# Value sums of the pooled attention from the local attention's value tiles, by 0/1 products on the tensor engine

## The chip, the cores and the metric

The kernel runs on one core of one Trainium2 chip. The metric is the device time of one execution in microseconds (us). Engines: PE multiplies matrices (PEld loads its weights), DVE is the vector engine, ACT the scalar engine, POOL the general engine, SP issues most transfers. Sixteen DMA engines move the data. Each engine works through its own instructions in a fixed order and waits on semaphores for the others.

## What is computed

All arrays are f32. Attention is computed twice, once on means of four neighbouring tokens ("pooled") and once inside a band of seven tokens ("local"). The sum of both goes through a Fourier mixing, a norm and a feed-forward layer.

```
q, k, v = (8, 8, 576, 64)                      # batch, heads, tokens, dim
q_d, k_d, v_d = means over 4 tokens             # 144 groups
out_d = softmax(q_d k_d^T / 8) v_d              # pooled
out_l = softmax(q k^T / 8 where |i - j| < 4) v  # local
x = repeat(out_d, 4) + out_l                    # as (8, 576, 512)
u = x + real(fft(fft(x, axis=1), axis=2))
y = u + relu(norm(u) @ w1) @ w2                 # w1 512 x 2048, w2 2048 x 512
```

## The kernel before, in words

The attention and the mixing (`Pooled`, `Unit`, `Mix`) run batch by batch over the first 300 us or so; the feed-forward part takes the rest and keeps PE full with its own weights. The eight batches overlap: each is paced 20 schedule units after the one before.

A batch's local attention is five `Unit`s of 128 token columns. Each loads `qkT` (queries and keys of all heads, 512 KB) and `vaug` (values with a column of ones, two windows of 64 tokens by four pairs of heads, 260 KB), scores it on PE, takes maxima on DVE, exponentials on ACT, turns the result on PE, copies it on ACT, multiplies by `vaug` (`values`, tile `av`) and divides on DVE (`result`).

The pooled attention of a batch (`Pooled`) works in three parts. Its queries and keys are sums over four columns of each `qkT` (`sum_in`, L526 on DVE; L523 and L524 on POOL for the keys of batches 2 to 7), 144 groups. Its values are the tile `vsum`: four slices of `in_vg_dram` (every fourth token of the values, once more in DRAM) loaded on top of one another, the first by a plain transfer of SP's queue, the other three by accumulating transfers that POOL issues (`sum_v`, L360). The 16 groups beyond 128 are then laid out by ACT in four copies to `vd` (`spread`, L365). `values` multiplies with both (L428 with `vd`, L441 with `vsum`, tile `avd`).

The order on every engine is written out by hand: the table `AT` gives each step a time in schedule units, `at(...)` files it, and the steps are emitted sorted by that time. The times only set the order. Waits come from data, from the buffers of each tile (`NUM_V`, `NUM_QKT`) and from PSUM banks, which `bank` hands out by the filed time of the step that reads them. Behind the attention in the order, but among it in time, run the loads of the first feed-forward blocks (`ul`, `um`, `ud` into `ut`, accumulated by POOL's transfers at L868 and L874) and the decode of the first weights (a load to `raw`, then ACT, POOL and three steps of DVE on `wt`, then a cast on ACT and a difference).

Of the kernel before, what the change touches and what calls it, by code (L numbers as in the profile page):

```python
# [17 lines left out]
NUM_V, NUM_QKT, NUM_P = 3, 6, 2  # L18
# [6 lines left out]
POOL_SUMS = ((slice(0, 4), 0), (slice(4, 8), 1))  # L25
AT = {
    "pooled": (1.39, -0.67, -3.4, -4.0, -3.53),
    "mix": (18.69, 18.25, 18.08),
    "local_steps": (0.47, 2.18, 2.55, 4.76, 5.66, 7.44, 8.16),
    "pooled_steps": (0.21, 1.79, 2.89, 4.92, 5.63, 7.66, 9.61),  # L30
    "qk": (-14.26, 2.19),
    "sums": (-2.08, 0.13),
    "sum_v": (-14.82, -12.57, -2.25, 2.01),
    "load_v": (-1.96, 4.03),
    "store_pooled": (1.06, 0.8, 3.47),
    "crosses": ((1, 4.16), (2, 6.77), (0, 9.01)),
    "folds": ((3, 3.9), (1, 5.14), (2, 8.37), (0, 10.61)),
    "splits": (0.74, 1.1, 1.97),
    "z": (9.21, 9.92, 13.29, 13.75),
    "sequence": (12.93, 2.04, 0.82, 1.85),  # L40
# [3 lines left out]
    "decode": (50.58, 9.93, 6.96, 1.15, 1.87),  # L44
    "decode_steps": (-1.32, -0.39, 0.86, 2.11, 2.49),
    "add0": (62.59, 0.41, 6.0),
    "early": (3.29, 3.77),
    "constants": (10.75, 29.61),
    "waves": ((16.5, 0.16), (17.55, 0.92), (22.14, 0.9)),
    "waves_c": ((21.38, -3.88), (23.72, -1.16), (25.3, 7.97)),  # L50
    "qk1": (-16.47, 3.04),
    "sum_v1": (-19.42, -12.25, -4.44, 3.9),
    "qk0": (-8.34, 1.63),
    "sums0": (-0.4, 0.38),
    "sums1": (-2.05, 0.32),
    "load_v0": (-2.76, 5.2),
    "load_v1": (1.5, 3.84),
    "sum_v0": (-13.22, -6.45, -4.68, 5.69),
    "units0": (-2.71, -1.19, 4.29, 12.25, 17.39),
    "norms0": (88.98, -2.44, 95.16, 4.13),  # L60
    "add1": (75.6, 5.23, 15.18),
    "norms1": (146.64, 4.24, 0.79, 1.83),
    "keep": (25.6,),
    "shift": (0.5,),
    "pace0": (1.04, 1.21),
    "parts": (0.22, 5.36, 9.32),
    "parts0": (5.14, 8.37, 13.06),
    "spread": (11.49, 5.0),
# [48 lines left out]
def kernel(  # L117
# [4 lines left out]
    vg: bass.AP,  # L122
# [5 lines left out]
    c_signs: bass.AP,  # L128
    out: bass.AP,
# [13 lines left out]
    LQ = 32  # L143
    NSL = 3
# [126 lines left out]
    vds = [pd.tile([P, 2, 2, D + 1], F32, name=f"vd{i}") for i in range(2)]  # L271
    for x in vds:
        nc.gpsimd.memset(x, 0.0)
# [11 lines left out]
        "values": "result",  # L285
        "sequence": "sequence_low",
# [60 lines left out]
    class Pooled:  # L347
# [40 lines left out]
        def exps(self, i):  # L388
# [3 lines left out]
            sd = self.sd[i] = pd.tile([P, 2, 2, G], F32, name="sd", bufs=1)  # L392
# [6 lines left out]
        def transpose_p(self, i):  # L399
# [5 lines left out]
            for k in range(4):  # L405
                x = sd[:, k % 2 if i else 0, k // 2, G - LQ :]
# [10 lines left out]
        def values(self, i):  # L417
# [19 lines left out]
            for a in range(2 if i else HP):  # L437
                for hl, o in enumerate(av):
# [5 lines left out]
                        self.vs[:, 2 * hp + hl, :],  # L444
# [5 lines left out]
        def result(self, i):  # L450
# [48 lines left out]
    class Unit:  # L499
# [1094 lines left out]
```

## Time and profile before

| | us |
|---|---|
| median of 3 runs | 1092.33 (1091.62 to 1097.79) |
| profiled execution, device time | 1091.27 |
| its span | 1089.5 |

| engine | busy us | share of the span |
|---|---|---|
| PE | 1037.6 | 95% |
| PEld | 855.9 | 79% |
| DVE | 755.4 | 69% |
| POOL | 591.0 | 54% |
| ACT | 488.1 | 45% |

The shares are means over unlike stages, so the kernel is read in stretches: the first 62 us, in which the pipeline of batches fills, five batches up to 249 us, the last two with their mixing, and the feed-forward part, which is PE's from about 348 us on. A busy PE is not PE at its peak, since its small products count with the time that each takes to pass through.

### The profile page before, as it was taken

To read this page: it belongs to the slowest core of one execution; us is meant where nothing else is said; L and a number is where in the kernel's file an instruction comes from. 1 tells how busy PE (TensorE), PEld (TensorE's weight loads), DVE (VectorE), ACT (ScalarE), POOL (GpSimd) and SP (SyncE) were. 2 spreads that over 40 slices of the span, in tenths; PEclk is the share of its full clock that TensorE was granted. 3 is DMA by queue.
4 is the path that set the end of the run, shared out by engine and by line. 5 is a ranking of instruction groups with operands and counts; after the bars stand their busy time and mean duration, and the time that the engine had idled before them with its cause. 6 is when DMAs were issued, how large, how long until landed. Compare 5 with 4: busy or idle time off the path is not lost.

```text
span 1089.5 us, 22339 instructions
## 1 busy us (share of the span) xinstructions
PE 1037.6 (95%) x8060; PEld 855.9 (79%) x8060; DVE 755.4 (69%) x1579; ACT 488.1 (45%) x1355; POOL 591.0 (54%) x742
## 2 busy tenths in 40 slices
PE   5899888989999999989999999999999999999998
PEld 4687767768887888878878888888888888888886
DVE  5888779988888997662566557678557668555544
ACT  4776656767554442111144333445334345333331
POOL 2254846653355674635646894457695448334330
PEclk7799799999999999999999999999999999999999
DMA  9797999885445442948832792223693223322212
GB/s 292 215 281 238 238 282 265 211 249 167 145 144 155 136 142 74 263 137 192 185 116 67 174 189 82 69 64 123 172 201 90 80 65 103 112 77 64 73 39 77
DMA packets 107880, 164.73 MB, mean 151 GB/s; under 512 B 13331, under 2 KB 56165, under 8 KB 107770
## 3 DMA queue, kind: packets, MB, share of 16 engines
q1 hardware_dynamic: 87850, 135.39, 38.5%
q0 software_dynamic: 19920, 27.92, 15.8%
q8 instruction: 63, 1.03, 0.4%
q14 instruction: 47, 0.39, 0.1%
HBM read 123.81 MB, written 39.19 MB: 150 GB/s over the span
## 4 chain that ended last, share of the span: by engine, by line
PE 72%; DMA 10%; DVE 7%; POOL 3%; ACT 3%; issue 3%; SPq 1%; DVEq 0%; POOLq 0%; ACTq 0%
PE acc L1211 24%; PE product L1165 21%; PE hps L962 10%; DMA vsum<-in_vg_dram 5%; PE acc L980 3%; PE acc L981 3%; PE acc L982 3%; DMA qkT<-in_qk_dram 2%; PE y L721 1%; PE tpn L919 1%; PE mix L767 1%; ACT sb L560 1%; PE avd L441 1%; DMA raw<-in_wq_dram 1%; DMA x<-rest 1%
## 5 line engine op out<-in xcount | busy, mean ns | idle before, releaser
L1211 PE MATMUL acc<-w,h 128*128 128x512 f32 x1152 | 288.4, 390 | 0.0
L1100 POOL TENSOR_TENSOR w<-w 128x256 fp32r<-128x256 f32 x168 | 187.0, 1300 | 163.8 <-ACT w L1096 151.4
L1211 PEld LDWEIGHTS acc<-w,h 128*128 128x128 f32 x1152 | 215.5, 188 | 44.4
L1216 DVE TENSOR_TENSOR ut<-acc,ut 128x512 f32<-128x512 f32 x96 | 66.1, 689 | 75.0 <-PE acc L1211 74.4
L1165 PE MATMUL product<-x_t,w 128*128 128x512 f32 x432 | 110.2, 390 | 0.6 <-ACT raw L1176 0.6
L1176 ACT COPY raw<-product 128x512 f32<-128x512 f32 x72 | 42.2, 586 | 139.5 <-PE product L1165 139.5
L962 PE MATMUL hps<-unT,w1h 128*128 128x512 f32 x384 | 103.2, 391 | 0.0
L1191 ACT ACTIVATE h<-raw 128x512 fp32r<-128x512 f32 x72 | 45.5, 632 | 125.9 <-DVE raw L1183 125.9
L1216 DVE TENSOR_TENSOR more_tokens<-acc,more_tokens 128x512 f32<-128x512 f32 x96 | 66.1, 688 | 43.6 <-PE acc L1211 42.3
L1165 PEld LDWEIGHTS product<-x_t,w 128*128 128x128 f32 x432 | 80.8, 188 | 18.2 <-ACT raw L1176 1.5
L1183 DVE TENSOR_TENSOR raw<-product,raw 128x512 f32<-128x512 f32 x72 | 49.6, 690 | 56.5 <-PE product L1165 30.2
L1118 POOL TENSOR_TENSOR w<-w,w 128x512 fp32r<-128x512 f32 x48 | 82.0, 1813 | 9.8 <-ACT w L1114 9.8
L962 PEld LDWEIGHTS hps<-unT,w1h 128*128 128x128 f32 x384 | 71.5, 188 | 14.6
L970 DVE SCALAR_TENSOR_TENSOR hl<-hps,hh 128x512 fp32r<-128x512 f32 x48 | 32.8, 685 | 65.1 <-ACT hh L966 65.1
L980 PE MATMUL acc<-w2h,hh 128*128 128x512 f32 x192 | 76.2, 397 | 0.7 <-DVE ut L986 0.7
L982 PE MATMUL acc<-w2h,hl 128*128 128x512 f32 x192 | 75.2, 392 | 0.0
L981 PE MATMUL acc<-w2l,hh 128*128 128x512 f32 x192 | 75.2, 392 | 0.0
L1165 PE MATMUL product<-x_b,w 128*128 128x512 f32 x288 | 73.3, 390 | 0.0
L1165 PE MATMUL product<-x_two,w 128*128 128x512 f32 x288 | 73.1, 390 | 0.0
L560 ACT ACTIVATE sb<-sc,mx 128x64 f32<-128x64 f32 x320 | 69.8, 329 | 1.3
L966 ACT ACTIVATE hh<-hps 128x512 fp32r<-128x512 f32 x48 | 28.3, 591 | 91.9 <-PE hps L962 91.9
L904 POOL TENSOR_TENSOR rstd<-rstd,mhalf 128x1 f32<-128x1 f32 x36 | 22.3, 618 | 84.3 <-DVE rstd L903 77.6
(176 smaller groups left out, 2313.4 us busy)
## 6 DMA issues: line engine op xcount, KB each, us to landing
w<-ws SPq DMA_DIRECT2D x168, 128.0 KB
qkT<-in_qk_dram SPq DMA_DIRECT2D x40, 512.0 KB
raw<-in_wq_dram SPq DMA_DIRECT2D x50, 256.0 KB
w<-ws SPq DMA_DIRECT2D x48, 256.0 KB
vaug<-in_vw_dram SPq DMA_DIRECT2D x40, 260.0 KB
ul<-x SPq DMA_DIRECT2D x8, 1024.0 KB
vsum<-in_vg_dram POOLq DMA_DIRECT2D x24, 325.0 KB, 7.5
out_dram<-ut SPq DMA_DIRECT2D x24, 256.0 KB
```

Source lines behind the costliest of these rows:

```text
L560: nc.scalar.activation(out=self.sb[:, hp, h2], in_=sc[:, hp], func=AF.Exp, scale=0.125, bias=self.mx[:, h2, hp : hp + 1],)
L962: nc.tensor.matmul(hps, a[:, c, :], unT[:, x, c, :], start=(i == 0), stop=(i == len(mms) - 1))
L980: nc.tensor.matmul(acc, hh, w2h, start=start, stop=False)
L981: nc.tensor.matmul(acc, hh, w2l, start=False, stop=False)
L982: nc.tensor.matmul(acc, hl, w2h, start=False, stop=stop)
L1100: nc.gpsimd.tensor_sub(out=w[:, HN:], in0=w[:, HN:].bitcast(F32), in1=w[:, :HN].bitcast(F32))
L1118: nc.gpsimd.tensor_sub(out=x, in0=x.bitcast(F32), in1=h.bitcast(F32))
L1165: nc.tensor.matmul(ps, w[:, a, c], x[:, b, c], start=begin and i == 0, stop=i == len(mms) - 1, skip_group_check=not begin,)
L1183: nc.vector.tensor_add(out=x, in0=self.ps[p, "z" if out == (0, 0) else "y"], in1=x)
L1191: nc.scalar.activation(out=self.hidden(p, out, 0), in_=x, func=AF.Relu)
L1211: nc.tensor.matmul(acc, a, b, start=n == 0, stop=n == len(mms) - 1)
L1216: nc.vector.tensor_add(out=u, in0=self.accs.pop((p, t)), in1=u)
```

## The change

The copy of the values in DRAM, its four transfers per batch and the four copies to `vd` go. Instead a constant `groups` (0/1, 160 KB) is loaded once; the step `group_values` multiplies it with the batch's five `vaug` tiles on PE, which gives sums over four tokens in three PSUM banks, and `copy_values` brings them to `vsum` on ACT. So that each `vaug` gives its own 32 groups, the pooled keys get 159 places in place of 144 (`KEY_SUMS`); a group that occurs twice gets values from one place and zeros at the other. All keys' sums of a batch are thus made for 159 places, and scores, maxima and exponentials are 159 wide. The five `vaug` of a batch are needed together, so there are five buffers (before: three) and they are loaded earlier (`load_v`). Most numbers of `AT` for the steps of the attention, the mixing and the first loads are new; of these only those of the replaced steps are shown.

```diff
-NUM_V, NUM_QKT, NUM_P = 3, 6, 2
+NUM_V, NUM_QKT, NUM_P = 5, 6, 2
...
-POOL_SUMS = ((slice(0, 4), 0), (slice(4, 8), 1))
...
-    "sum_v": (-14.82, -12.57, -2.25, 2.01),
-    "load_v": (-1.96, 4.03),
+    "load_v": (-11.565, 4.0),
+    "groups": (10.6, 11.771),
...
-    vds = [pd.tile([P, 2, 2, D + 1], F32, name=f"vd{i}") for i in range(2)]
-    for x in vds:
-        nc.gpsimd.memset(x, 0.0)
+    groups = pd.tile([P, NPAIR, 2, LQ], F32, name="groups")
+    nc.sync.dma_start(out=groups.rearrange("p m n g -> p (m n g)"), in_=c_groups)
+    none = pd.tile([P, LQ], F32, name="none")
+    nc.gpsimd.memset(none, 0.0)
...
-        def sum_v(self, r):
-
-            if r == 0:
-                self.vs = pd.tile([P, H + 2, D + 1], F32, name="vsum", bufs=2)
-            eng = nc.gpsimd if r else nc.sync
-            how = {"accum_op": ALU.add} if r else {}
-            eng.dma_start(out=self.vs.rearrange("g h d -> g (h d)"), in_=vg[self.b, r], **how)
-
-        def spread(self):
-            for k in range(4):
-                r = slice(k * LQ, k * LQ + LQ)
-                nc.scalar.copy(out=vds[self.b % 2][r, :, k % 2], in_=self.vs[r, H:])
+        def group_values(self):
+
+            vas = [u.va for u in units[NPAIR * self.b : NPAIR * self.b + NPAIR]]
+            ps = self.vps = [bank("vsum")[:, : HP * (D + 1)] for _ in range(3)]
+            for n2 in range(2):
+                for k, m in enumerate(GROUP_UNITS[:4]):
+                    for h2 in range(2):
+                        r = slice(h2 * D, h2 * D + D)
+                        nc.tensor.matmul(
+                            ps[h2][k * LQ : k * LQ + LQ],
+                            groups[r, m, n2],
+                            vas[m][r, n2].rearrange("p h d -> p (h d)"),
+                            start=n2 == 0,
+                            stop=n2 == 1,
+                            skip_group_check=True,
+                        )
+            m = GROUP_UNITS[4]
+            for i in range(2):
+                for n2 in (0, 1, None):
+                    for a in range(2):
+                        for h2 in range(2):
+                            r, k = slice(h2 * D, h2 * D + D), 2 * h2 + a
+                            c = (D + 1) * (2 * i + (1 - a if n2 is None else a))
+                            nc.tensor.matmul(
+                                ps[2][k * LQ : k * LQ + LQ, c : c + D + 1],
+                                none[r] if n2 is None else groups[r, m, n2],
+                                vas[m][r, n2 or 0, 2 * i + a, :],
+                                start=n2 != 1,
+                                stop=n2 != 0,
+                                skip_group_check=True,
+                            )
+
+        def copy_values(self):
+            vs = self.vs = pd.tile([P, 3, HP, D + 1], F32, name="vsum", bufs=1)
+            for i, ps in enumerate(self.vps):
+                nc.scalar.copy(out=vs[:, i].rearrange("p h d -> p (h d)"), in_=ps)
...
-            s = sums[self.b]
+            q, k = sums[self.b]
             sps = self.sps[i] = [
-                bank("sp")[:, : (2 if i else 1) * G].rearrange("p (a g) -> p a g", g=G) for _ in range(2)
+                bank("sp")[:, : (2 if i else 1) * GK].rearrange("p (a g) -> p a g", g=GK) for _ in range(2)
             ]
             for a in range(2 if i else HP):
                 for hl, sp in enumerate(sps):
                     r = slice(hl * D, hl * D + D)
                     if i:
                         hp = 2 * i - 2 + a
-                        nc.tensor.matmul(sp[:, a, :], s[r, 0, hp, :P], s[r, 1, hp, :], start=True, stop=True)
+                        nc.tensor.matmul(sp[:, a, :], q[r, hp, :P], k[r, hp, :], start=True, stop=True)
                     else:
                         nc.tensor.matmul(
-                            sp[a * LQ : a * LQ + LQ, 0, :], s[r, 0, a, G - LQ :], s[r, 1, a, :], start=True, stop=True
+                            sp[a * LQ : a * LQ + LQ, 0, :], q[r, a, G - LQ :], k[r, a, :], start=True, stop=True
                         )
...
-            vd = vds[self.b % 2]
+            vd = self.vs[:, 2]
...
-                    v = vd[r, i - 1] if i else vd[r, a // 2, a % 2]
+                    v = vd[r, 2 * i - 2 : 2 * i] if i else vd[r, a]
...
-                        self.vs[:, 2 * hp + hl, :],
+                        self.vs[:, hl, hp, :],
...
-            times_v = AT[f"sum_v{b}" if b < 2 else "sum_v"]
-            for r in range(4):
-                at(pooled_at(b) + times_v[r], self.sum_v, r)
-            at(pooled_at(b) + AT["spread"][min(b, 1)], self.spread)
+            for d, fn in zip(AT[f"groups{b}" if b < 2 else "groups"], (self.group_values, self.copy_values)):
+                at(pooled_at(b) + d, fn)
...
-                sums[self.b] = pd.tile([P, 2, HP, G], F32, name="sums", bufs=1)
-            x = self.qkT.rearrange("p i h w -> p (i h) w")
-            to = sums[self.b].rearrange("p i h g -> p (i h) g")
-            for at0, g, n in SUMS[self.m]:
-                groups = x[:, :, at0 : at0 + 4 * n].rearrange("p h (g r) -> p h g r", r=4)
-                for h, pool in POOL_SUMS:
-                    if pool and self.b in POOL_BATCHES:
+                sums[self.b] = [
+                    pd.tile([P, HP, n], F32, name=f"sums_{x}", bufs=1) for x, n in (("q", G), ("k", GK))
+                ]
+            for i, places in enumerate((SUMS, KEY_SUMS)):
+                x, to = self.qkT[:, i], sums[self.b][i]
+                for at0, g, n in places[self.m]:
+                    four = x[:, :, at0 : at0 + 4 * n].rearrange("p h (g r) -> p h g r", r=4)
+                    if i and self.b in POOL_BATCHES:
                         two = p2.tile([P, HP, 32, 2], F32, name="two", bufs=1)[:, :, :n]
-                        nc.gpsimd.tensor_tensor(out=two, in0=groups[:, h, :, 0:2], in1=groups[:, h, :, 2:4], op=ALU.add)
-                        nc.gpsimd.tensor_tensor(out=to[:, h, g : g + n], in0=two[:, :, :, 0], in1=two[:, :, :, 1], op=ALU.add)
+                        nc.gpsimd.tensor_tensor(out=two, in0=four[:, :, :, 0:2], in1=four[:, :, :, 2:4], op=ALU.add)
+                        nc.gpsimd.tensor_tensor(out=to[:, :, g : g + n], in0=two[:, :, :, 0], in1=two[:, :, :, 1], op=ALU.add)
                     else:
-                        nc.vector.tensor_reduce(out=to[:, h, g : g + n], in_=groups[:, h], axis=AX.X, op=ALU.add)
+                        nc.vector.tensor_reduce(out=to[:, :, g : g + n], in_=four, axis=AX.X, op=ALU.add)
...
+    groups = np.zeros((2, W, 5, 2, 32))
+    for k, m in enumerate(GROUP_UNITS):
+        taken = {}
+        for at0, first, n in KEY_SUMS[m]:
+            for g in range(n):
+                tokens = [SPANS[m][at0 + 4 * g + r] for r in range(4)]
+                taken.setdefault(min(tokens) // 4, (first + g - (P - 1 if k == 4 else k * 32), tokens))
+        for g, (slot, tokens) in taken.items():
+            if g in MINE[m]:
+                n2 = min(n for n in range(2) if set(tokens) <= set(SPANS[m][STARTS[m][n] :][:W]))
+                for t in tokens:
+                    groups[:, SPANS[m][STARTS[m][n2] :].index(t), m, n2, slot] = 1.0
+    groups = groups.reshape(P, -1)
...
+MINE = [range(0, 30), range(30, 58), range(58, 87), range(87, 115), range(115, 144)]
+KEY_SUMS = [[(0, 0, 32)], [(0, 32, 32)], [(0, 128, 16), (65, 144, 15)], [(0, 64, 32)], [(0, 96, 32)]]
+GROUP_UNITS = (0, 1, 3, 4, 2)
 SUMS = [[(0, 0, 32)], [(16, 32, 28)], [(12, 60, 12), (65, 129, 15)], [(0, 99, 30)], [(4, 72, 27)]]
```

Where the instructions stand now. First SP, at the program's start: `ident` and `mask` are constants, `qkT` and `vaug` the loads of the first units. Before:

```order
L191 DMA ident<-in_c_ident_dram 128x128
L264 DMA raw<-in_c_mask_dram 128x128
L360 DMA vsum<-in_vg_dram 128x650
L506 DMA qkT<-in_qk_dram 128x1024 x4
L510 DMA vaug<-in_vw_dram 128x520
L506 DMA qkT<-in_qk_dram 128x1024
L360 DMA vsum<-in_vg_dram 128x650
L510 DMA vaug<-in_vw_dram 128x520
L506 DMA qkT<-in_qk_dram 128x1024 x2
L510 DMA vaug<-in_vw_dram 128x520
```

Now, the same place:

```order
L190 DMA ident<-in_c_ident_dram 128x128
L263 DMA raw<-in_c_mask_dram 128x128
L271 DMA groups<-in_c_groups_dram 128x320
L527 DMA qkT<-in_qk_dram 128x1024 x4
L531 DMA vaug<-in_vw_dram 128x520
L527 DMA qkT<-in_qk_dram 128x1024
L531 DMA vaug<-in_vw_dram 128x520
L527 DMA qkT<-in_qk_dram 128x1024
L531 DMA vaug<-in_vw_dram 128x520
L527 DMA qkT<-in_qk_dram 128x1024
L531 DMA vaug<-in_vw_dram 128x520
L527 DMA qkT<-in_qk_dram 128x1024
```

The first slices of `vsum` for two batches are gone, and the fifth `vaug` (one row further) stands behind eight loads of `qkT`.

Second PE, in the fourth batch: `sp`, `tp` and `avd` are the pooled scores, their transposes and the pooled result, `mix` the mixing of an earlier batch, `av` the local result. Before:

```order
L767 MATMUL mix<-chanm,yl 128x258
L767 MATMUL mix<-chanm,yh 128x258 x2
L767 MATMUL mix<-chanm,yl 128x258
L767 MATMUL mix<-signs,yz 128x258
L589 MATMUL av<-vaug,pT 64x65 x16
L428 MATMUL avd<-vd_149,ptd_2245 32x65 x8
L441 MATMUL avd<-vsum,ptd_2243 32x65 x8
```

Now:

```order
L402 MATMUL sp<-sums_k,sums_q 128x159 x4
L429 MATMUL tp<-ident,sd 128x128 x2
L432 MATMUL tp<-ident,sd 32x128 x4
L363 MATMUL vsum<-vaug,groups 32x260 x16
L378 MATMUL vsum<-vaug,groups 32x65 x8
L378 MATMUL vsum<-vaug,none 32x65 x4
L378 MATMUL vsum<-vaug,groups 32x65 x8
L378 MATMUL vsum<-vaug,none 32x65 x4
L611 MATMUL av<-vaug,pT 64x65 x16
L767 MATMUL yz<-seqm,z 2x290 x8
L453 MATMUL avd<-vsum,ptd_2505 32x65 x8
L466 MATMUL avd<-vsum,ptd_2503 32x65 x8
```

The 40 new products stand one local `av` and one mixing product ahead of the first pooled result that needs them; everything behind them on PE waits with them for the batch's fifth `vaug`.

Third POOL, in the fifth batch: `ut` are token loads of the first feed-forward block, `two` and `sums` the keys' sums, `wt` a decode step. Before:

```order
L221 TENSOR_SCALAR wt<-wt 128x256
L868 DMA ut_110<-ud_57 128x1x512
L360 DMA vsum<-in_vg_dram 128x650
L523 TENSOR_TENSOR two<-qkT 128x256
L524 TENSOR_TENSOR sums<-two 128x4x32
L868 DMA ut_111<-ud_57 128x1x512
L523 TENSOR_TENSOR two<-qkT 128x4x56
```

Now:

```order
L220 TENSOR_SCALAR wt<-wt 128x256
L896 DMA ut_113<-um_73 128x2x256
L890 DMA ut_110<-ud_57 128x1x512
L545 TENSOR_TENSOR two<-qkT 128x256
L546 TENSOR_TENSOR sums_k<-two 128x4x32
L890 DMA ut_111<-ud_57 128x1x512
L545 TENSOR_TENSOR two<-qkT 128x256
```

The accumulating transfer of `vsum` is gone from between them; the sums are 128 x 256 wide for every unit but the third.

## Rows read from the trace of the kernel before

**Rows 1.** Stretches: length, busy us of each engine (instructions), PE clock, DMA share, GB/s

```profile
0.00:62.00 62.00, 45.72 (x861) 35.05 (x862) 41.97 (x131) 40.69 (x145) 21.40 (x36) 0.78 0.86 251
62.00:249.00 187.00, 164.87 (x2873) 135.85 (x2874) 157.19 (x481) 126.59 (x464) 110.72 (x167) 0.95 0.91 252
249.00:278.70 29.70, 28.80 (x505) 23.89 (x504) 26.12 (x89) 22.80 (x85) 11.60 (x16) 1.00 0.48 145
180.00:200.00 20.00, 15.92 (x305) 12.91 (x294) 19.05 (x57) 13.22 (x47) 11.44 (x15) 1.00 0.96 272
```

The engines stand in the order PE, PEld, DVE, ACT, POOL.

**Rows 2.** The page's chain that ended last, shares of the span by engine

```profile
PE 72%; DMA 10%; DVE 7%; POOL 3%; ACT 3%; issue 3%; SPq 1%; DVEq 0%; POOLq 0%; ACTq 0%
```

**Rows 3.** DMA queues, 0 to 310 us: packets, MB, share; issues, KB, us to landing

```profile
q1 hardware_dynamic: 29430, 58.39, 55.9%
q0 software_dynamic: 7504, 13.24, 25.4%
...
vsum<-in_vg_dram POOLq DMA_DIRECT2D x24, 325.0 KB, 7.5
...
vsum<-in_vg_dram SPq DMA_DIRECT2D x8, 325.0 KB
```

**Rows 4.** Chain of waits, 0 to 100 us: start, us, what

```profile
1.65 3.14 DMA vsum<-in_vg_dram
...
22.53 4.89 DMA vsum<-in_vg_dram
```

**Rows 5.** Chain of waits, 100 to 260 us, same columns

```profile
97.29 8.99 DMA raw<-in_wq_dram
...
173.60 6.69 DMA qkT<-in_qk_dram
...
182.38 8.45 DMA vsum<-in_vg_dram
190.85 0.30 ACT vd L365
```

**Rows 6.** Waits of DVE and ACT, 62 to 249 us: us in total, times, longest

```profile
DVE wt L229 <- POOL wt L221: 6.5, 3, 2.9
DVE w2l L251 <- ACT w2h L246: 4.8, 2, 3.0
DVE sums L526 <- DMA qkT<-in_qk_dram: 4.3, 3, 1.7
...
DVE w1l L251 <- ACT w1h L246: 0.9, 1, 0.9
...
ACT vd L365 <- DMA vsum<-in_vg_dram: 6.6, 4, 3.0
```

**Rows 7.** Instructions by shape, 62 to 249 us; L526: one line, min/median/max ns

```profile
L386 DVE TENSOR_REDUCE mxd<-sp 128x2 f32<-128x288 f32 x20 | 8.1, 445 | 0.0
L386 DVE TENSOR_REDUCE mxd<-sp 128x1 f32<-128x144 f32 x10 | 2.5, 295 | 0.0
L365 ACT COPY vd<-vsum 32x130 f32<-32x130 f32 x20 | 6.0, 298 | 6.7 <-DMA vsum<-in_vg_dram 6.6
L395 ACT ACTIVATE sd<-sp,mxd 128x144 f32<-128x144 f32 x50 | 15.2, 381 | 0.5
L773 ACT COPY o<-mix 128x258 f32<-128x258 f32 x10 | 4.0, 398 | 0.0
L526 DVE TENSOR_REDUCE sums<-qkT x60: 336/605/676, 8.5 to 253.4; 128x128 f32<-128x512 f32 x10, 128x112 f32<-128x448 f32 x10, 128x48 f32<-128x192 f32 x10, 128x60 f32<-128x240 f32 x10
```

**Rows 8.** Small products on PE: chain rows, then timeline rows, start, us, shape

```profile
237.45 1.26 PE sp L377 x8
255.85 0.41 PE sp L379 x16
195.71 0.40 PE L428 MATMUL avd<-vd,ptd 64*32 64x65 f32 x16
196.03 0.39 PE L441 MATMUL avd<-vsum,ptd 128*32 128x65 f32 x11
```

More of the change, by code (lines that the diff above doesn't have):

```diff
@@ L24 @@
 PACE = 20
-POOL_SUMS = ((slice(0, 4), 0), (slice(4, 8), 1))
 AT = {
[L27 to L32, printed above, removed]
-    "sum_v": (-14.82, -12.57, -2.25, 2.01),
-    "load_v": (-1.96, 4.03),
[L35 to L40, printed above, removed]
+    "pooled": (1.39, -1.682, -3.279, -4.179, -3.53),
+    "mix": (18.504, 17.944, 18.064),
+    "local_steps": (0.745, 1.871, 2.694, 4.76, 5.66, 7.44, 8.214),
+    "pooled_steps": (0.946, 1.778, 2.89, 4.92, 5.63, 7.863, 9.169),
+    "qk": (-13.864, 2.19),
+    "sums": (-1.884, 0.239),
+    "load_v": (-11.565, 4.0),
+    "groups": (10.6, 11.771),
+    "store_pooled": (1.06, 2.553, 3.47),
+    "crosses": ((1, 4.16), (2, 6.524), (0, 9.01)),
+    "folds": ((3, 3.843), (1, 5.114), (2, 8.459), (0, 10.61)),
+    "splits": (0.74, 1.175, 1.966),
+    "z": (9.21, 10.197, 12.281, 13.303),
+    "sequence": (12.804, 2.04, 0.954, 1.943),
     "mixed": (21.86, 2.32, 0.37, 0.44, 1.73, 2.55),
@@ L43 @@
     "ffn": (2.14, 1.64),
[L44 to L47, printed above, removed]
+    "decode": (50.58, 9.93, 8.429, 1.15, 1.87),
+    "decode_steps": (-1.32, -0.304, 0.86, 2.11, 2.73),
+    "add0": (61.253, 1.204, 6.32),
+    "early": (3.061, 4.713),
     "constants": (10.75, 29.61),
[L49 to L63, printed above, removed]
+    "waves": ((15.301, 0.16), (17.286, 0.92), (20.944, 2.831)),
+    "waves_c": ((20.094, -5.127), (23.72, 2.255), (27.466, 7.97)),
+    "qk1": (-21.509, 3.04),
+    "groups1": (10.6, 11.544),
+    "qk0": (-8.402, 1.336),
+    "sums0": (-0.4, 0.469),
+    "sums1": (-5.128, 0.365),
+    "load_v0": (-4.18, 2.691),
+    "load_v1": (-9.0, 4.333),
+    "groups0": (12.057, 12.6),
+    "units0": (-4.673, -1.19, 4.29, 12.25, 17.39),
+    "norms0": (92.56, -2.44, 93.504, 4.13),
+    "add1": (84.678, 5.23, 15.674),
+    "norms1": (139.931, 4.201, 3.347, 1.845),
+    "keep": (25.544,),
     "shift": (0.5,),
     "pace0": (1.04, 1.21),
-    "parts": (0.22, 5.36, 9.32),
-    "parts0": (5.14, 8.37, 13.06),
-    "spread": (11.49, 5.0),
+    "parts": (4.6, 8.372, 12.084),
+    "parts0": (5.14, 8.37, 11.66),
 }
@@ L128 @@
     c_signs: bass.AP,
+    c_groups: bass.AP,
     out: bass.AP,
@@ L143 @@
     LQ = 32
+    GK = P + LQ - 1
     NSL = 3
@@ L285 @@
         "values": "result",
+        "group_values": "copy_values",
         "sequence": "sequence_low",
@@ L391, in exps @@
             nc.scalar.mul(out=mx, in_=mx, mul=2.0**-7)
-            sd = self.sd[i] = pd.tile([P, 2, 2, G], F32, name="sd", bufs=1)
+            sd = self.sd[i] = pd.tile([P, 2, 2, GK], F32, name="sd", bufs=1)
             for hl, sp in enumerate(self.sps[i]):
@@ L405, in transpose_p @@
             for k in range(4):
-                x = sd[:, k % 2 if i else 0, k // 2, G - LQ :]
+                x = sd[:, k % 2 if i else 0, k // 2, GK - LQ :]
                 nc.tensor.matmul(rest[k * LQ : k * LQ + LQ, 0], x, ident, start=True, stop=True)
@@ L454, in result @@
             for hl, o in enumerate(av):
-                nc.vector.tensor_scalar(
-                    out=rs[:, hl], in0=o[:, :, D], scalar1=1e-9, scalar2=4.0, op0=ALU.add, op1=ALU.mult
-                )
+                nc.vector.tensor_scalar_add(out=rs[:, hl], in0=o[:, :, D], scalar1=4e-9)
             nc.vector.reciprocal(out=rs, in_=rs)
@@ L1496, in _constants @@
     signs[[0, 1, 32, 33]] = [1.0, -1.0]
-    out = {"c_ident": ident, "c_mask": mask, "c_seq": seq, "c_chan": chan, "c_signs": signs}
+    groups = np.zeros((2, W, 5, 2, 32))
[11 more added lines that the diff above has]
+    groups = groups.reshape(P, -1)
+    out = {"c_ident": ident, "c_mask": mask, "c_seq": seq, "c_chan": chan, "c_signs": signs, "c_groups": groups}
     out = {n: np.ascontiguousarray(a, dtype=np.float32) for n, a in out.items()}
@@ L1533, in _arrays @@
     both = np.pad(both, [(0, 0)] * 5 + [(0, pad)])
+    both[..., SEQ:] = both[..., SEQ - pad : SEQ][..., ::-1]
     data["qk"] = np.stack([both[..., s] for s in SPANS], axis=1).reshape(B, NPAIR, P, -1)
@@ L1539, in _arrays @@
     data["vw"] = np.pad(rows, [(0, 0)] * 6 + [(0, 1)], constant_values=1).reshape(B, NPAIR, P, -1)
-    groups = v.reshape(B, HEADS, 2, SEQ // 8, 4, DIM)
-    groups = np.concatenate([groups[:, :, 0], groups[:, :, 1, ::-1]], axis=2)
-    groups = np.pad(groups, [(0, 0)] * 4 + [(0, 1)], constant_values=0.25)
-    rest = np.zeros((B, HEADS, 32, 4, DIM + 1), groups.dtype)
-    rest[:, :, 16:] = groups[:, :, P:]
-    rest = rest.reshape(B, 2, 2, 2, 32, 4, DIM + 1).transpose(0, 5, 3, 2, 4, 1, 6).reshape(B, 4, P, 2, DIM + 1)
-    groups = np.concatenate([groups[:, :, :P].transpose(0, 3, 2, 1, 4), rest], axis=3)
-    data["vg"] = groups.reshape(B, 4, P, -1)
     w1, w2 = (np.asarray(inputs[n]) for n in ("moe_w_ch1", "moe_w_ch2"))
```

1 line of the change is left out of this document (removed).

## The prediction

> **What bounds the kernel now.** I read the stretches first [rows 1]. The whole change lies in the attention stage, so the reader should look at three of them. In the first 62 us (up to the first batch's local store) nothing is near full except the DMA engines, 0.86 busy. In the next 187 us, five batches at 187 / 5 = 37.4 us each, three things are close together: DMA 0.91, PE 164.9 / 187 = 0.88, DVE 157.2 / 187 = 0.84. The batch from 249 to 278.7 us is the useful comparison: its loads are over, DMA falls to 0.48, and a batch takes 29.7 us with PE at 28.8 / 29.7 = 0.97. So the middle batches are held back by something that the late batch does not have, and loads are the first suspect. The chain of the whole program gives DMA 10% [rows 2], and half of that is the transfers of `vsum`, the value sums that the change removes.
>
> Next the DMA queues of the first 310 us [rows 3]. The accumulating transfers are issued by POOL on q0: 13.24 MB there take 25.4% of 310 us, that is 78.7 us of all 16 engines, or 5.94 us per MB. On q1 58.39 MB take 55.9%, 173.3 us, or 2.97 us per MB. An accumulated megabyte costs twice a plain one.
>
> Then where these transfers are waited for. The first batch's four follow one another from 1.65 us to 22.53 + 4.89 = 27.4 us [rows 4]. Later, one piece of the chain is an 8.45 us `vsum` transfer that ends at 190.83 us and releases the four copies to `vd` [rows 5]. But the wait table of the middle [rows 6] shows how little of such a piece is idle time: ACT waits 6.6 us in four times for `vsum`. DVE, the engine with the least slack besides PE, waits 4.3 us for `qkT`, 6.5 us for the decode step of POOL and 4.8 + 0.9 us for ACT's decode casts. I count these 16.5 us as late transfers seen at second hand: a `raw` transfer of 256 KB took 8.99 us to land [rows 5], POOL issues accumulating transfers between the decode steps, and ACT's casts stand behind the `vd` copies. That is where I chose; only the 4.3 us end on a transfer directly.
>
> **The change, part by part.** *Transfers.* Per batch four of 128 x 650 x 4 bytes = 0.333 MB go. Eight plain ones cost 8 x 0.333 x 2.97 = 7.9 us of DMA time, 24 accumulating ones 24 x 0.333 x 5.94 = 47.5 us. The new table `groups`, 128 x 320 x 4 = 0.164 MB, costs 0.5 us. So 55 us of DMA time go, 6.9 per batch, of about 0.91 x 37.4 = 34 us. DMA stops being close to a bound; what a free engine is worth is set by what is late next.
>
> *Start.* The five `vaug` tiles take over from the four `vsum` transfers. Two plain and three accumulating transfers left the first 22 us: 2 x 0.333 x 2.97 + 3 x 0.333 x 5.94 - 0.5 = 7.4 us of DMA time. The group products must wait for the fifth `vaug`, which now stands behind eight `qkT` loads. I take about half, -4 us (bounds 0 and -8).
>
> *Middle.* All 16.5 us of DVE idle time above are taken as recovered. Bounds: 4.3 us, the direct wait, and 187 - 157.2 / 0.95 = 21.5 us, where DVE would be as full as from 180 to 200 us (19.05 of 20) [rows 1].
>
> *New work on PE.* Per batch 16 products of 64 x 32 by 260 columns and 24 by 65 columns. The trace counts each f32 product twice. Eight products of 64 x 32 by 144 columns (x16) took 0.41 us; eight by 65 columns ran from 195.71 to the next group at 196.03, 0.32 us, or 0.04 each [rows 8]. By columns the 16 cost 0.41 x 2 x 260 / 144 = 1.5 us, at most; scaled by the slope between the two rows, (0.41 - 0.32) / 8 / 79 per column, they cost 16 x (0.051 + 116 x 0.00014) = 1.1 us. I take 1.3, and 24 x 0.04 = 0.95 for the small ones: 2.25 us a batch, 18 in all. The far bound is the pace of the wide 64 x 128 products, four in 1.26 us for 144 columns [rows 8]: (16 x 260 + 24 x 65) x 1.26 / 4 / 144 = 12.5 us a batch, which the shape makes unlikely; I keep 4.5 us (twice mine) as bound. In the start PE idles 16 us of 62, which hides two batches' worth. In the middle five batches bring 11.3 us and PE idles 22 us; with PE at 0.88 I put half on the path, +5.6. In the late, PE-full stretch one batch counts whole, +2.3. The Trainium skill (TensorEngine Tiling, Gotcha 1: PSUM Pressure) says that row tiles of different halves cannot use one PSUM bank at the same time; the small products of both halves write one bank, where the measured rows used two. By that rule they would cost about 0.95 us a batch more, half of it on the path, and the sum would be near 1081; no row before shows it.
>
> *DVE.* Ten maxima per batch get 159 columns for 144. Two against one segment is 445 - 295 ns for 144 columns [rows 7], 1.04 ns a column, so 10 x 15 x 1.04 = 0.16 us a batch, 1.3 us in all. In batches 0 and 1 the twelve sums of keys grow by 15/144: 12 x 0.605 x 0.104 = 0.8 us [rows 7]. Together +2, on the path since DVE is nearly full.
>
> *ACT.* Four `vd` copies at 298 ns, 1.19 us, become three copies of 128 x 260, priced like `o`, 128 x 258 at 398 ns: 1.19 us. Nothing. Ten exponentials get 15 more columns; 144 take 381 ns, so at most 10 x 15 x 381 / 144 = 0.4 us a batch, hidden by ACT's idle 60 us of 187. If ACT had no slack it would cost 3 us.
>
> *POOL and the buffers.* POOL loses 24 issues and gains a tenth in the key sums of six batches. It idles 76 us of 187, so nothing; were it full, the two would roughly cancel. The wait for `vsum` on ACT becomes a wait for PE. Three PSUM banks per batch are held between products and copies, one and a bit schedule units, among some fifty bank uses; I price that at nothing (bounds 0 to 2 us).
>
> *PE's clock.* In the middle the mean granted clock is 0.95 [rows 1]. It has two levels, 1.2 and 2.4 GHz, so PE spent 2 x 0.05 x 187 = 18.7 us at the lower one and lost half of that, 9.4 us of work; in the late batch, where PE idles 0.9 us, it is 1.00. If some of the 22 us of PE's idle time go, some of the 9.4 us comes back: I take -4 (bounds 0 and -9.4).
>
> *Order.* The moved times of the other steps have no row that prices them: 0, bounds -6 to +6.
>
> **Sum.** The profiled execution took 1091.27 us (span 1089.5 and 1.8 around it), 1.1 below the median of the runs. -4 (start) - 16.5 (DVE's idle time) + 5.6 + 2.3 (PE) + 2 (DVE) - 4 (clock) = -14.6, so 1077 us.
>
> **Rivals.** *More* (chance 0.20). With DMA out of the way DVE runs at 0.95 in the middle: (157.2 + 1.5) / 0.95 = 167, -20, and the start gives its -8: 1063 us. For it speaks the late batch, 29.7 us at low DMA. Against it: that batch decodes little and sums no keys.
>
> *The transfers were hidden anyway* (0.18). Only the direct wait goes, -4.3 and -2 at the start; the new work stays, +5.6 + 2.3 + 2, and the clock stays as it is: 1095 us. For it: ACT's waits for `vsum` are 6.6 us in all and 3.0 at most [rows 6], however long the transfer on the chain.
>
> *Slower* (0.12). The group products stand in PE's fixed order, and with them everything behind waits for the batch's fifth `vaug`. By the table this is loaded at 4 x 4.0 - 11.565 = 4.4 and used at 10.6 - 3.53 = 7.1 units after the batch begins, 2.6 units of 37.4 / 20 = 1.87 us, so 5 us. A `qkT` of 512 KB took 6.69 us to land, a `raw` of 256 KB 8.99 us [rows 5]. At 8.99 PE would stand 4 us in each of seven batches: 1077 + 28 = 1105 us. It cancels the gain from 14 / 7 = 2 us of wait per batch. Against it: those landings were measured with the DMA engines full.
>
> **How the numbers follow.** The forecast, 1077 us, has chance 0.50 and its own range 1068 to 1086. Range 1060 to 1097: all of the forecast, most of *more* (0.14) and of *hidden* (0.15), together about 0.8; the slower case and the far end of *more* stay out. A change of under 1% is about what a measurement of this kernel cannot tell from none; the border is 1081.4. Faster: 0.20 from *more* and three quarters of the forecast, 0.38, so 0.58. Slower: 0.09 of the slower case and 0.02 of the hidden one, 0.11. Same: the rest, 0.31.
>
> **What would show it.** Right: DMA busy near (0.91 x 187 - 5 x 6.9) / 174 = 0.78 in the middle, q0 at 13.24 - 8 = 5.2 MB, batches of 33 to 35 us, PE at 0.95 there, hardly any DVE wait on POOL's decode step. Products of `vsum` at 2 to 2.5 us a batch confirm the PE price. Wrong: DMA down and batches still at 37 us (hidden); PE waiting for `vaug` in front of the group products (slower); the first batch's store still near 62 us says that the start was not the transfers'. After 348 us nothing should change but the offset.

## The result and the profile after

The changed kernel took 1077.67 us (median of four runs, 1077.20 to 1080.11) against 1092.3 us before: ratio 0.986, 95% interval 0.9825 to 0.9895. A second set of six runs gave 1078.41 us and 0.9863 (0.9833 to 0.9893). So it is 1.4% faster, 14.6 us, and the forecast was 1077 us, 14.6 us down. The agreement is too good: several terms of the sum were wrong, and their errors cancelled, as the stages show.

Both profiled executions of the changed kernel are the longest of their sets (1080.11 and 1079.88 us), while the profiled one of before was 1.1 us under its median. Between the profiled spans there are therefore only 11.2 us to find (1089.5 to 1078.3).

The stretches of the kernel after, cut at the same places as [rows 1]: start, five middle batches, one late batch, the last batch. Columns: length, busy us of PE, PEld, DVE, ACT, POOL (instructions), PE clock, DMA share, GB/s.

```profile
0.00:60.10 60.10, 51.21 (x1044) 38.74 (x1048) 46.40 (x138) 42.98 (x153) 16.74 (x32) 0.80 0.65 226
60.10:238.50 178.40, 167.41 (x3251) 136.33 (x3244) 153.74 (x473) 121.95 (x446) 97.86 (x148) 0.98 0.78 222
238.50:268.40 29.90, 29.53 (x582) 24.46 (x584) 27.36 (x89) 21.34 (x79) 10.16 (x14) 1.00 0.41 132
268.40:287.80 19.40, 19.40 (x318) 17.44 (x315) 13.76 (x51) 11.78 (x43) 3.71 (x6) 1.00 0.30 100
```

The middle went from 187.0 us to 178.4, with DMA down from 0.91 to 0.78 and PE up from 0.88 to 167.41 / 178.4 = 0.94. DVE idles 24.7 us there, before 29.8. The late batch did not get shorter (29.7 to 29.9 us).

The DMA queues of the first 300 us (packets, MB, share of 16 engines), as in [rows 3]:

```profile
q1 hardware_dynamic: 28333, 55.73, 56.5%
q0 software_dynamic: 4048, 5.25, 10.3%
```

q0 fell from 13.24 to 5.25 MB. The transfers are gone as counted, and the page's chain (shares of the span) says the same: DMA 10% in [rows 2] is 3% now, PE 72% is 78%.

```profile
PE 78%; DVE 11%; issue 3%; DMA 3%; ACT 2%; SPq 2%; POOL 1%; DVEq 0%; POOLq 0%; ACTq 0%
```

What DVE waits for in the middle, 55 to 240 us (us in total, times, longest), against [rows 6]:

```profile
DVE rs L626 <- PE av L611: 7.5, 6, 2.1
DVE rsd L480 <- PE avd L466: 2.9, 5, 1.1
DVE mxd L411 <- PE sp L402: 2.7, 3, 1.3
...
DVE sums_q L548 <- DMA qkT<-in_qk_dram: 0.5, 1, 0.5
```

The waits on POOL's decode step (6.5 us before), on ACT's casts (4.8 + 0.9) and on `qkT` (4.3) are gone or small. In their place stand waits for PE: `av`, `avd` and `sp`, 13.1 us. DVE's idle time changed its cause more than its size.

The new products at full clock, two rows of the chain of waits (start, us, what): 16 wide products (L363, counted twice) and 24 small ones (L378).

```profile
222.49 1.04 PE vsum L363 x32
223.53 0.68 PE vsum L378 x48
```

That is 1.72 us, where 2.25 were forecast, but it is the quickest of the five middle batches. The slowest ran from its first product at 77.12 us to PE's next step at 79.61, 2.49 us (start, us, what):

```profile
77.12 1.66 PE L363 MATMUL vsum<-vaug,groups 64*32 64x260 f32 x30
...
79.61 0.70 PE L611 MATMUL av<-vaug,pT 64*64 64x65 f32 x32
```

Read in this way the five took about 2.1 us in the mean, 1.9 in the second profile (without waits in between), near the forecast.

### The profile page after: what moved, and what is told of

Its sections match the earlier page's. It is cut to its first block, busy times and chain, and to the rows that moved or that the text cites. A ratio compares the mean times of both kernels' runs of the same rounds, so it can differ in the third digit from the quotient of the medians.

```text
span 1078.3 us, 23547 instructions
## 1 busy us (share of the span) xinstructions
PE 1047.1 (97%) x8700; PEld 860.7 (80%) x8700; DVE 762.7 (71%) x1579; ACT 486.5 (45%) x1347; POOL 571.7 (53%) x717
## 4 chain that ended last, share of the span: by engine, by line
PE 78%; DVE 11%; issue 3%; DMA 3%; ACT 2%; SPq 2%; POOL 1%; DVEq 0%; POOLq 0%; ACTq 0%
PE acc L1233 24%; PE product L1187 21%; PE hps L984 8%; PE y L743 4%; PE acc L1002 3%; PE acc L1004 3%; PE acc L1003 3%; PE tpl L594 2%; PE av L611 2%; PE mix L789 1%; PE avd L466 1%; PE sc L563 1%; PE tpn L941 1%; PE sp L402 1%; PE tp L429 1%
## 5 line engine op out<-in xcount | busy, mean ns | idle before, releaser
L1122 POOL TENSOR_TENSOR w<-w 128x256 fp32r<-128x256 f32 x168 | 182.5, 1233 | 165.1 <-ACT w L1118 152.7
L1205 DVE TENSOR_TENSOR raw<-product,raw 128x512 f32<-128x512 f32 x72 | 49.6, 689 | 55.6 <-PE product L1187 30.5
L1218 DVE SCALAR_TENSOR_TENSOR h<-raw,h 128x512 fp32r<-128x512 f32 x72 | 64.3, 893 | 1.0 <-ACT h L1213 0.7
```

Source lines behind the costliest of these rows:

```text
L1122: nc.gpsimd.tensor_sub(out=w[:, HN:], in0=w[:, HN:].bitcast(F32), in1=w[:, :HN].bitcast(F32))
L1205: nc.vector.tensor_add(out=x, in0=self.ps[p, "z" if out == (0, 0) else "y"], in1=x)
L1218: nc.vector.scalar_tensor_tensor(out=l, in0=x, scalar=0.0, in1=h.bitcast(F32), op0=ALU.max, op1=ALU.subtract)
```

## The experiments

Here are the stages of all profiled executions, cut at the local stores of the first, the sixth and the last batch (us). One profile each; the two of the changed kernel differ by 1.6 us in the start and 2.7 us in the middle, so smaller differences say nothing.

| kernel | start | five middle batches | last two | rest | ratio to before, 95% |
|---|---|---|---|---|---|
| before | 62.0 | 187.2 | 48.0 | 792.3 | 1 |
| after | 60.1 | 178.4 | 49.3 | 790.5 | 0.986 (0.9825–0.9895) |
| after, again | 61.7 | 175.7 | 49.2 | 791.5 | 0.9863 (0.9833–0.9893) |
| transfers back | 68.9 | 190.6 | 49.1 | 791.7 | 1.0049 (1.0027–1.0070) |
| half the bytes back | 67.5 | 179.4 | 49.2 | 792.2 | 0.9986 (0.9963–1.0010) |
| before, 8 of 32 transfers | 66.0 | 175.7 | 48.2 | 791.6 | 0.9913 (0.9884–0.9943) |
| products in one batch | 59.0 | 175.3 | 49.6 | 791.1 | 0.9828 (0.9795–0.9862) |
| products twice | 60.7 | 187.6 | 51.1 | 793.9 | 1.0024 (1.0003–1.0046) |
| change, old order | 63.8 | 191.7 | 52.9 | 792.2 | 1.0068 (1.0036–1.0100) |
| before, new order | 63.5 | 187.0 | 49.1 | 790.5 | 1.0002 (0.9976–1.0027) |
| change, old times of computing steps | 60.8 | 187.0 | 52.6 | 790.9 | 1.0000 (0.9983–1.0018) |
| change, old times of loads, sums, decode | 67.2 | 191.1 | 47.4 | 796.4 | 1.0083 (1.0056–1.0110) |
| change, more on POOL | 59.2 | 175.7 | 49.4 | 789.9 | 0.9835 (0.9808–0.9863) |
| products in one batch, more on POOL | 54.8 | 175.1 | 49.5 | 791.7 | 0.9803 (0.9779–0.9827) |

**The transfers back, for nobody.** To the change the 32 old transfers are added, into a scratch that no one reads.

```diff
+        def idle_load(self, r):
+            if r == 0:
+                self.idle = dram.tile([P, 656], F32, name=f"idle{self.b}")
+            eng = nc.gpsimd if r else nc.sync
+            how = {"accum_op": ALU.add} if r else {}
+            eng.dma_start(out=self.idle[:, :650], in_=vg[self.b, r], **how)
```

> The changed kernel with the 32 transfers of the old value sums put back at their old times and on their old queues (8 plain, 24 accumulating, 0.333 MB each), but into a scratch tensor in DRAM that no engine reads, so nobody waits for them. The theory of the prediction (the transfers cost by keeping the DMA engines busy, and other loads come late): DMA share of the middle back above 0.9, waits for qkT and for decode steps back, half of the gain or more lost, 1085 to 1093 us. The rival (only the wait of ACT for vsum and the old order held the kernel back): at most 2 us, 1076 to 1080 us, whatever the DMA share.

Measured 1101.49 us, 1.9% above the change, about 20 us, and more than the 1085 to 1093 us expected. Stretches of it, start and middle (columns as above), and three waits from 68.9 to 259.5 us:

```profile
0.00:68.90 68.90, 51.20 (x1028) 39.18 (x1032) 46.76 (x137) 42.24 (x151) 22.28 (x39) 0.85 0.82 250
68.90:259.50 190.60, 170.41 (x3259) 137.81 (x3260) 159.28 (x474) 123.08 (x449) 111.40 (x164) 0.97 0.91 243
```

```profile
DVE rs L636 <- PE av L621: 10.8, 8, 5.4
...
PE vsum L371 <- DMA vaug<-in_vw_dram: 5.1, 3, 2.4
```

DMA is back at 0.91 in the middle and the batches at 190.6 / 5 = 38.1 us; start and middle pay, the rest does not. So transfers that no one waits for cost time, and the rival by which they were hidden anyway falls. But the 20 us are not their price in the kernel of before: PE now waits 5.1 us for `vaug` in front of the group products in the middle and 6.1 us in the start. That is the wait of the slower rival. In the two profiles of the change PE waits nothing and 0.8 us for `vaug` in front of the products, from 0 to 300 us.

**Half the bytes, the same number of transfers.** As in the experiment before, but half the columns, into one SBUF buffer, with the second batch's first two and last transfers at other times.

```diff
+                self.idle = pd.tile([P, 325], F32, name="idle", bufs=1)
...
+            eng.dma_start(out=self.idle, in_=vg[self.b, r][:, :325], **how)
```

> The changed kernel with half of each old transfer (325 of 650 columns) put back on the old queues, into a scratch tile in SBUF that no engine reads; the second batch's are a few units later than of old. If the loss of the last such run (1.9%) came from the time of the DMA engines and of the queues: a third to two thirds of it, 0.992 to 0.998 of before. If it came from the writing to DRAM: at most 0.988.

Measured 1092.1 us, 1.2% above the change and just over the range expected: by the total, half the bytes cost two thirds. That reading does not hold, as the queue of SP shows (waits from 0 to 70 us).

```profile
SPq L361 <- DMA idle<-in_vg_dram: 11.7, 2, 10.2
```

The single buffer makes the second batch's first transfer wait on SP for the first batch's last one, and the loads behind it wait too, so its start of 67.5 us has a cause of its own. In the middle it took 179.4 us with DMA at 0.88, 1.0 to 3.7 us above the change, where the whole bytes took 190.6 with DMA at 0.91. All of POOL's issues are made here too (POOL is busy 112.0 us in the middle, 97.9 and 97.7 in the change), so POOL's time for them is not what cost 12 to 15 us there. The two runs differ in the bytes and also in where they are written, SBUF here and DRAM there; which of the two makes the cost rise so steeply is not shown, and what half the bytes cost in the start stays open.

**Before without most transfers.** The old kernel and order, no group products; batches 2 to 7 use the first two batches' sums, so only 8 of the 32 transfers are made.

```diff
         def spread(self):
+            self.vs = pooleds[self.b % 2].vs
...
-            for r in range(4):
+            for r in range(4) if b < 2 else ():
```

> The kernel before with the transfers of the value sums made for the first two batches alone (8 of 32); the other six batches use those two sums, so their pooled result is left out in effect. No group products, and the order of before. The theory that the transfers' time on the DMA engines held the kernel back, in any order: 6 of 8 batches gain, 0.983 to 0.988 of before. The rival that the last runs suggest (the old order cannot use the freed engines; change and order pay only together): 0.995 or more.

Measured 1083.83 us against 1093.41, -9.5 us, between the two expectations. The middle falls by 11.5 us to 175.7 us; the start is 4.0 us longer, at a lower PE clock (0.72, before 0.78), for a reason that no run shows. Waits of DVE in the middle:

```profile
DVE wt L229 <- POOL wt L221: 6.4, 3, 2.6
...
DVE w2l L251 <- ACT w2h L246: 1.2, 1, 1.2
```

The casts (5.7 us before) and `qkT` (4.3 before, 0.2 here) follow the transfers, as forecast. The wait on POOL's decode step does not: 6.5 us with the transfers, 6.4 without. It belongs to the old order, as the run with the new order alone, further down, confirms.

**Old order under the change, and new order without it.** In the first, all old times but those of the new steps, of the `vaug` loads and of the pooled parts 1 and 2; in the second, all new times but those of the `vaug` loads. Three of the numbers, for the first:

```diff
-    "mix": (18.504, 17.944, 18.064),
-    "qk": (-13.864, 2.19),
-    "sums": (-1.884, 0.239),
+    "mix": (18.69, 18.25, 18.08),
+    "qk": (-14.26, 2.19),
+    "sums": (-2.08, 0.13),
```

> The changed kernel with the order of before: all times of the steps are those of before, except for the new steps, the loads of vaug and the times of the pooled parts 1 and 2, which cannot stand before the new products. The theory of the prediction priced the order at 0, bounds -6 and +6: 1072 to 1084 us. The rival (the new order carries the gain): 1088 us or more.

> The kernel before, transfers and vd copies kept, with the new times of all steps that it shares with the change (not the loads of vaug). The theory of the prediction: the time of before within 6 us, 1086 to 1098. The rival (the order carries the gain): 1076 to 1082 us.

The change with the old order took 1101.34 us, 2.1% or 22 us above the change; the old kernel with the new order 1095.1 us, no difference. In the first, PE waits from 63.8 to 255.5 us are these; in the middle of the change the first is 0.2 us, the second nothing, and the third nothing (0.2 us in the second profile):

```profile
PE sc L557 <- ACT sb L582: 5.7, 7, 1.2
PE tp L432 <- ACT ptd L439: 3.4, 5, 0.7
PE vsum L363 <- DMA vaug<-in_vw_dram: 2.0, 2, 1.7
```

So the order is worth nothing alone and the change needs it. The second run says two things more. The first is what DVE waits for in its middle, 63.5 to 250.5 us:

```profile
DVE w2l L251 <- ACT w2h L246: 5.5, 2, 3.5
DVE sums L526 <- DMA qkT<-in_qk_dram: 4.1, 5, 1.3
```

The wait on POOL's decode step (`wt`) is not among its waits: the new order takes it away with all transfers in place, while the casts and `qkT` stay. The second: its last two batches take 49.1 us, like the change's 49.3, with none of the new work. So what the last two batches lost, 1.2 to 1.3 us, comes with the order alone too.

**Which half of the order?** The change with the old times of the computing steps only (local and pooled steps, mixing, sequence), and with the old times of the rest (loads, sums, decode, norms).

```diff
-    "local_steps": (0.745, 1.871, 2.694, 4.76, 5.66, 7.44, 8.214),
+    "local_steps": (0.47, 2.18, 2.55, 4.76, 5.66, 7.44, 8.16),
```

> The changed kernel with the old times of the computing steps alone (local and pooled steps, mixing, folds, splits, sequence, the first batch's parts); loads, sums, constants, decode and first norms keep the new ones. The old order as a whole cost the change 2.05% (1.0068 against 0.9863). If that lies in how PE's and DVE's steps of neighbouring batches are interleaved: 0.998 to 1.005 of before here, and at most 0.992 in the next run. If it lies in the loads and their neighbours: at most 0.990 here.

> The other half: the old times of the loads of qkT, the sums, constants, stores of the pooled result, start of the units and of the pooled parts, decode and first norms; the computing steps keep the new ones. If the 2% lie here: 0.997 to 1.005 of before; if in the computing steps: at most 0.992; if only both orders together work, more than 0.995 in both runs.

Measured 1094.15 us (+1.4%) and 1104.24 us (+2.2%). Each half alone loses the whole gain or more, and the second adds 5 to 7 us in the start and 5 to 6 us in the rest. The numbers of the table hold only together. This has a limit: each of these kernels mixes two tables, so how much of the 22 us is the new order's merit, and how much the harm of mixing, stays open.

**The products' price, from both sides.** Products made in the first batch only (later batches use its sums), and products made twice.

```diff
+            self.vs = pooleds[0].vs
...
+            if b == 0:
+                for d, fn in zip(AT["groups0"], (self.group_values, self.copy_values)):
+                    at(pooled_at(b) + d, fn)
```

```diff
-            for n2 in range(2):
+            for n2 in (0, 1, 0, 1):
...
-                for n2 in (0, 1, None):
+                for n2 in (0, 1, None, 0, 1, None):
```

> The changed kernel with the group products and their copies made in the first batch alone; the other seven batches use the first batch's value sums, so their pooled result is left out in effect. The theory of the prediction put 5.6 + 2.3 us of these products on the path: about 1070 us. If PE were the bound all through, seven batches at the traced 1.7 to 2 us each would come back, 12 to 14 us: 1064 us. If the products lie in PE's idle time: 1076 us or more.

> The changed kernel with every group product issued twice (the sums over the second pass are doubled on nothing else: the second pass starts each sum anew, so the values stay). Leaving seven of eight out gave 3.5 us back. If half hides in PE's idle time, as the prediction put it, 8 x 1.75 / 2 = 7 us are added, 0.992 of before; if PE is the bound throughout, 14 us, 0.999; if idle time hides nearly all, at most 0.989.

Without seven batches of products, 7 x 1.72 = 12 us of PE even at the quickest, the kernel is 0.35% faster, 3.8 us, and the intervals overlap. With eight more it is 1.6% slower, 17.6 us, above all three expectations. One batch's double set in its chain of waits (start, us, what):

```profile
232.34 1.91 PE vsum L363 x64
234.25 1.36 PE vsum L378 x96
```

That is 1.91 + 1.36 - 1.72 = 1.55 us more, only 12.4 us for eight. Waits from 60.7 to 248.3 us of the kernel with doubled products:

```profile
DVE rs L626 <- PE av L611: 20.0, 9, 3.8
...
PE vsum L378 <- issue: 5.6, 3, 2.4
```

DVE's wait for `av`, which stands right behind the products, went from 7.5 to 20.0 us. PE also stopped three times within the products without anything that the profile shows. Taking products away returns little: in the kernel with one batch of products PE's busy time falls to 161.0 us in the middle, and the middle to 175.3 us only. Its row:

```profile
59.00:234.30 175.30, 161.01 (x2865) 131.75 (x2865) 155.09 (x475) 119.15 (x437) 98.46 (x149) 0.95 0.81 226
```

The clock in this row took part of the relief. Some 10 us of products are gone from the middle (5 x 2.1), but PE is busy only 4.7 to 6.4 us less than in the two profiles of the change, and its clock is 0.95 where they have 0.98 and 0.99. By the working of the forecast, half of the time at the lower of the two levels is lost: 8.8 us of work here, 3.6 and 1.8 there, an estimate from these rows. PE waits more in this kernel, and its clock is low behind such waits. One of them and the stretch that follows (length, busy us of PE, clock, DMA share, GB/s):

```profile
110.00:115.00 5.00, 1.39 (x16) 0.94 0.89 253
115.00:120.00 5.00, 5.00 (x95) 0.72 1.16 269
```

Whether the middle would be shorter at the higher clock no run shows.

**The change once more:**

> The changed kernel itself, beside the others on this chip: 0.986 of before by every theory (0.983 to 0.990).

Measured 1078.41 us, ratio 0.9863.

**What is late next.** DVE is relieved, alone and with the products of one batch only: the second batch's keys' sums and the first low parts go to POOL.

```diff
-POOL_BATCHES = (2, 3, 4, 5, 6, 7)
+POOL_BATCHES = (1, 2, 3, 4, 5, 6, 7)
...
-LOW_ON_VECTOR = (0,)
+LOW_ON_VECTOR = ()
```

> The changed kernel with work moved from DVE to POOL, which lost 24 issues by the change: the low half of the first fold's split in all batches (8 x 0.69 us on DVE) and the keys' sums of the second batch (some 3.5 us). Leaving the group products out gave 3.5 us of 12, so something else is late next. If that is DVE: 0.978 to 0.983 of before. If PE is: 0.985 to 0.989. If POOL's slower steps come late: above 0.990.

> As the last, and the group products of seven batches left out as well (their pooled result is left out in effect). If PE and DVE bound the middle by turns, relief of both gives more than the sum of the two alone (3.5 us and what the last run gives): 0.970 to 0.977 of before. If the order itself or the loads are late next: 0.979 or more.

Measured 1075.85 us (0.9835) and 1072.93 us (0.9803). The first is 3.1 us better than the change by the ratios, with overlapping intervals: perhaps a little faster than both kernels, not settled. The second adds the two gains (0.35% + 0.28% would give 0.980) and no more, so the theory that PE and DVE hold each other, each relief worth little until both are made, falls. Its gain is mostly in the start, 54.8 us; the middle, with 6 to 7 us less on PE and 3 us less on DVE than in the two profiles of the change, stays at 175.1. First its row of the middle, then two waits of 58 to 232 us:

```profile
54.80:229.90 175.10, 160.02 (x2865) 130.84 (x2865) 150.69 (x470) 118.90 (x437) 104.79 (x158) 0.96 0.81 226
```

```profile
PE yz L769 <- DVE z L734: 6.5, 3, 3.0
PE yz L769 <- DVE rs L628: 3.6, 1, 3.6
```

Five different kernels have a middle of 175 to 176 us with PE between 158.6 and 165.8 us busy and DVE between 150.0 and 155.5. With neither engine full and DMA at 0.78 to 0.81, no single engine's load holds it there; PE's waits for `z` and `rs`, 10.1 us in this last run, are one place in which steps wait for each other. What decides stays open.

## Why the prediction was right in sum and wrong in its terms

*What bounds the middle, and the transfers.* Right: full DMA engines held the middle batches back. Taking the transfers away gives 11.5 us there in the old kernel, putting them back costs 12 to 15 us in the new. DMA's 0.78 and q0's 5.2 MB came as worked out (0.78 and 5.25); the batches of 33 to 35 us came at 35.7 and, in the second profile, 35.1 us.

*Middle, -16.5 us of DVE idle time.* Too large. The step that failed is "I count these 16.5 us as late transfers seen at second hand". For the casts and `qkT`, 10.0 us together, it held. The 6.5 us on POOL's decode step did not come from the transfers: the run with 8 of 32 kept 6.4 us of them, and the old kernel with the new order, all transfers made, has none. And of what was freed part went to waits for PE. DVE idles 24.7 and, in the second profile, 22.0 us (175.7 - 153.75), 5 to 8 us less. That DVE's wait on POOL is gone in the change is thus its order's doing.

*PE's products, +7.9.* The price came near in the mean, 1.9 to 2.1 us a batch in the middle against 2.25, and 1.72 at the quickest. What was taken wrong is the share on the path: their absence gives 3.8 us, half the term, and a second set costs 17.6. The late batch's whole +2.3 does not show when the products go: without them the last two batches take 49.6 us, with them 49.3. Added work counts there all the same: the second set makes them 51.1. The Trainium skill (TensorEngine Tiling, Gotcha 1: PSUM Pressure) states that different row tiles cannot access the same PSUM bank at the same time. No cost of it shows here: the small products of both halves write one bank, and at the quickest 24 of them took 0.68 us, 28 ns each, less than the 40 ns of the row that I priced them by [rows 8].

*Start, -4.* Measured -1.9 and -0.3. The fifth `vaug` was not the trouble (at most 0.8 us of waiting in front of the products). The stretch varies by some 2 us between profiles, and it was 66.0 us in the old kernel with 8 of 32 transfers, so what is left of the term is hardly to be told from nothing.

*PE's clock, -4.* The clock did rise, from 0.95 to 0.98 and 0.99. As a price it is not supported: the old kernel with the new order had 0.90 there and took the same 187.0 us. Nor does PE's busy share of the middle tell the clock: at 0.92 busy it was 0.95 with the products in one batch and 1.00 with half the bytes back. A gain of its own is not shown.

```profile
63.50:250.50 187.00, 164.99 (x2827) 133.58 (x2820) 157.24 (x473) 122.83 (x451) 110.50 (x164) 0.90 0.91 249
```

*DVE, +2.* About half. Start and middle together went from 42.0 + 157.2 to 46.4 + 153.7 us, 0.9 more (1.4 in the second profile). The maxima cost 0.8 us in the middle (10.7 before, 11.5 in the second profile), as worked out. ACT's copies, three at 410 ns, cost nothing, as forecast.

*Order, 0 with bounds of 6.* The mis-sized term. With the old times the change loses 22 us, and with half of them 15 or 24. The order was set for the new work; pricing the work on a fixed order and the order at nothing hid that the first needs the second. With the old order, as it was run here, the result is on the other side: 0.7% slower.

*Rivals.* *Hidden anyway*: refuted by the transfers put back. *Slower*: the wait for `vaug` in front of the products is at most 0.8 us in the change and 11 us once the DMA engines are full again; the reason given against it, that the landings were measured with full engines, was the right one. *More*: DVE was to run at 0.95 with the middle at 167; it runs at 0.86 to 0.88, and 13.1 us of its idle time in the first profile ends on late results of PE. Its sum also left out the late batch's +2.3.

The middle's terms (-16.5 + 5.6 - 4, and 1 of the 2 on DVE) made -13.9, measured -8.8 and -11.5. The late batches lost 1.2 to 1.3 us where 2.3 were charged, the start gave less than 4. The stages of the profiles thus sum to -11.2 and -11.4; that the medians lie 14.6 and 15.0 apart comes from where the profiled executions stood among their runs.

## What to carry to other kernels

Transfers that nobody seems to wait for still cost time when the DMA engines are near 0.9 busy: count their engine time, accumulating ones double, and try it by putting them back into a scratch. With an order set by hand, price a change and its order as one thing, since either alone may be worth nothing or less. And the price of added work is not the gain of removing it: the same products cost 17.6 us when doubled and gave 3.8 when taken away, with PE's clock lower as PE waited more.

## What was not expected of the hardware

PE's stops with nothing to wait for. From 50 to 300 us, PE's waits named `issue`, in which it waits for nothing that the profile shows, are none before, and these after (us, times, longest):

```profile
PE av L611 <- issue: 2.0, 1, 2.0
PE sc L563 <- issue: 1.7, 1, 1.7
PE tp L432 <- issue: 0.2, 1, 0.2
```

They are none with products in one batch, and 8.3 us with doubled ones, in or up to 5 us behind the rows of small products (all but the stop of 0.2 us above). The DMA queue of kind "instruction" carries 36 packets in the first 300 us before, 41 after and 46 with doubled products. That PE waits there for its own instructions is my reading; no run tested it, and the record speaks in part against it. With the old order the changed kernel has 40 packets and the same products, but only 0.2 us of such stops, and the old kernel with 8 of 32 transfers, 36 packets and no products, stops for 1.4 us in front of `avd`. Whatever their cause, the stops account for why doubling cost more than the products' own time: 5 x 1.55 us more products (1.91 + 1.36 - 1.72 a batch in its chain of waits) and 8.3 - 3.9 = 4.4 us more of such stops in the middle, 12.2 us, beside 9.2 and 11.9 measured.

POOL is busy for each accumulating transfer that it issues: fifteen in the middle of the kernel before, and fifteen of half the bytes in the experiment (mean ns behind the comma).

```profile
L360 POOL DMA_DIRECT2D vsum<-in_vg_dram x15 | 17.9, 1190 | 4.8 <-DMA vsum<-in_vg_dram 3.3 <-PE sp L377 1.3
```

```profile
L361 POOL DMA_DIRECT2D idle<-in_vg_dram x15 | 17.4, 1159 | 2.8 <-DMA idle<-in_vg_dram 2.7
```

With the whole bytes into the DRAM scratch they took less:

```profile
L361 POOL DMA_DIRECT2D idle<-in_vg_dram x15 | 14.9, 993 | 6.2 <-DMA idle<-in_vg_dram 3.3 <-PE mix L799 2.3 <-issue 0.3
```

So POOL pays 1.0 to 1.2 us for each, and half the bytes saved next to nothing: 17.9 us of POOL's time in the middle that the change takes away (POOL as a whole lost 12.9 there).
